# A seam of two matmul schedules reordered, kept sums weighed in pieces, and the last group's W2 sums moved from GpSimd to VectorE

## The chip, the core and the metric

The kernel runs on one core of a Trainium2 chip. Its engines work side by side, each on its own stream of instructions: TensorE (PE, the matmuls, with the loading of weights shown apart as PEld), VectorE (DVE), ScalarE (ACT), GpSimd (POOL) and SyncE (SP), which here only starts transfers (DMAs). GpSimd starts DMAs too, among them those that add what they carry to their target. The metric is the device time in microseconds (us) of one execution, as a median of several runs.

## The reference

Two layers follow each other, all in fp32. The first is attention with a polynomial sketch in place of the softmax; B, H, S, D are 4, 4, 1088, 32 and r is 8:

```python
def phi(x):                      # 64 features of a row
    a = np.einsum('rd,bhsd->bhsr', S1, x)
    b = np.einsum('rd,bhsd->bhsr', S2, x)
    return np.einsum('bhsi,bhsj->bhsij', a, b).reshape(*x.shape[:-1], r * r)
kv = np.einsum('bhsf,bhsd->bhfd', phi(k), v);  z = phi(k).sum(2)
x = (phi(q) @ kv) / (phi(q) @ z + 1e-6)        # as 4352 rows of 128
```

The second is a mixture of E = 8 experts without dropping: every row of x goes through every expert, and a matrix P (4352 x 8) weighs the results. P is the exponential of the gate's logits, normalized 8 times over experts and over rows (Sinkhorn):

```python
for e in range(E):               # w1[e]: 128 x 1024, w2[e]: 1024 x 128
    out += P[:, e:e+1] * (np.maximum(x @ w1[e], 0) @ w2[e])
```

P is never negative, so a row may be weighed before the relu (x times P) as well as after W2. The kernel uses both.

## The kernel before, in words

**Groups, items, blocks.** x lies transposed in SBUF (xT, 128 x 4352). Its columns are cut into groups (line 711), and a group with an expert is an *item*; an item is worked in *blocks*, each a share of the 1024 hidden features. The first eight groups run on experts 0 and 1 alone, unweighed, while attention and the routing are still being worked; their results are *kept* (kept0, kept1), to be weighed once P is there. Then come five groups of three tiles of 256 columns, with 7 experts each (6 for one of them), of two blocks an item, and a last group of two tiles of 256 columns, columns 0 to 511, with experts 2 to 7 and four blocks an item.

**Fewer multiplications.** Each block has two layers of matmuls, the *first products* (W1 times x, then a relu into hidden tiles hb or hx) and the *second products* (W2 times hidden, added up in four PSUM banks s). Both replace full products by fewer products of sums of their operands, and the sums are made by the other engines:
- Plain blocks (functions two, four; first products line 1058, relu on ScalarE line 1062; second products seven or twenty through into, matmul line 1434). Their sums of hidden tiles are VectorE's: lines 1077 (two tiles) and 1144 (three). In groups of two tiles, W2's sums ws (sums_of_two, lines 202 to 205) are four subtractions or additions of GpSimd per expert. In groups of three tiles W2's 20 forms are made once per expert, stored to HBM and loaded back (ws<-ws, 1280 KB).
- *New blocks* (function middle): all groups of three tiles but the first. Here the first products too work on sums: of W1 (forms wl and wf, made once per expert in forms_of_first, lines 271 to 325, and stored) and of x. A new x has two tiles, xe and de: VectorE weighs xT by a row of P spread over all partitions (px; line 806), ScalarE copies (line 815), and four adding DMAs of GpSimd join the halves (line 822; of these de<-xe and de<-de come first). A product is a *half product*: 64 rows of the array, 64 columns at a time, so that two different ones, one in the lower and one in the upper rows, run at once when they meet; a *whole* product fills all 128 rows. In a new block ScalarE copies a seed (line 1268), makes m5 (1270) and relus (1274); VectorE adds (1279).

**Order.** TensorE and VectorE, and ScalarE where the three-tile groups begin, run in the order in which the program is written (manual_schedule), up to the end of the new blocks; SyncE's transfers and GpSimd's instructions keep that order where keep_in_program_order says so, and are placed by the scheduler otherwise. Outside the new blocks the order comes from a generator (steps) that goes step by step: one step is one first product and the second products that are due, some 1.1 us in the three-tile group; beside (line 1454) hangs further work on steps c of an item, and prepare_new (line 1478) prepares the first two new items, with c counted from the first new item's start (negative is before). In the new blocks it comes from a list of jobs with planned times: block n begins at n x 8.83 (PERIOD, line 1222), and every job stands at its own time after it (FIRST, SCALAR, VECTOR, SECOND); jobs are sorted by time and written in that order. A block's second products stand some 13 to 25 us after its beginning. So at the *first seam*, in front of the new blocks, the second products of the last two plain blocks stand among the first products of the first new ones; at the *second seam*, behind them, the first products of the last group's first three blocks (EARLY) stand among the last second products. From there on the generator goes on with the last group.

**Kept outputs.** weigh_kept (line 827) is called at the beginning of an item, one part each: GpSimd weighs kept0 in pieces of 256 columns by a row of P (pb; line 771 in weigh), then kept1 if that group has it, then adds the second to the first (line 839), and for the last group subtracts one half from the other (line 842). Only the group at column 512 and the last group have a kept1. The last group's are done during the last new group.

**Forms of the next expert.** During the first three-tile group forms_of_first of the next expert is spread over the steps of an item: ScalarE copies and turns signs (line 279: turn), GpSimd adds by DMA (line 282: plus, wa<-wa and others), SyncE stores (line 285: keep_to, wf<-wa). ScalarE's turn_across at step 6 reads what the adding DMA wa<-wa brings; last_sum, the last addition, is at step 9.

## Time and profile before

Three runs took 902.21, 905.29 and 906.96 us; the median is 905.29. One more execution was profiled: it took 905.74 us, with a span of 904.0 us from first to last instruction. All times of the trace are of that one.

| | whole span | 110 to 310 us (plain blocks) | 310 to 335 (first seam) | 335 to 800 (new blocks) | 800 to 826 (second seam) | 826 to 904 (last group) |
|---|---|---|---|---|---|---|
| TensorE busy, us | 887.58 | 199.78 | 21.40 of 25 | 463.51 of 465 | 23.12 of 26 | 72.84 of 78 |
| VectorE busy | 776.84 | 167.56 | 11.06 | 440.28 | 21.86 | 52.19 |
| ScalarE busy | 551.58 | 126.69 | 11.17 | 316.70 | 11.71 | 36.41 |
| GpSimd busy | 192.50 | 23.42 | 6.88 | 108.03 | 13.20 | 17.77 |

How to read the rows of the profile: a window's row gives its length, then for PE, PEld, DVE, ACT and POOL the busy time with the count of instructions, then TensorE's granted clock (1.00 is full speed), the share of time in which the DMA engines were busy, and GB/s. A row of the timeline gives the time in the span, the duration, engine, line of the program, operation, what is written and from what, shapes, the number of instructions put together (x), and in brackets the idle time of the engine just before and what ended it. A row of the list of waits gives engine, target, line, what was waited for, and total, count and longest. SPq and POOLq rows are issues of DMAs; q1 is the queue of DMAs that SyncE starts, q0 that of GpSimd's. TensorE's busy time counts a lone half product, or two of them side by side, as busy alike.

### The profile page before, as it was taken

To read this page: it belongs to the slowest core of one execution; us is meant where nothing else is said; L and a number is where in the kernel's file an instruction comes from. 1 tells how busy PE (TensorE), PEld (TensorE's weight loads), DVE (VectorE), ACT (ScalarE), POOL (GpSimd) and SP (SyncE) were. 2 spreads that over 40 slices of the span, in tenths; PEclk is the share of its full clock that TensorE was granted. 3 is DMA by queue.
4 is the path that set the end of the run, shared out by engine and by line. 5 is a ranking of instruction groups with operands and counts; after the bars stand their busy time and mean duration, and the time that the engine had idled before them with its cause. 6 is when DMAs were issued, how large, how long until landed. Compare 5 with 4: busy or idle time off the path is not lost.

```text
span 904.0 us, 26768 instructions
## 1 busy us (share of the span) xinstructions
PE 887.6 (98%) x10934; PEld 608.3 (67%) x10934; DVE 776.8 (86%) x1525; ACT 551.6 (61%) x1251; POOL 192.5 (21%) x255
## 2 busy tenths in 40 slices
PE   8999999999999999999999999999999999999997
PEld 6777544456555447767777777777777777755775
DVE  7678689889878749999999998999989999989755
ACT  3355465576666646666767666767667676655443
POOL 3121100022111222411221221222122213132430
PEclk9999999999999999999999999999999999999999
DMA  9998200348877776865777678667776775641430
GB/s 253 304 281 291 60 1 1 88 106 235 270 206 219 204 192 183 242 189 170 189 227 214 160 178 242 203 164 205 212 187 180 228 205 154 177 149 39 124 93 13
DMA packets 84522, 159.13 MB, mean 176 GB/s; under 512 B 27936, under 2 KB 56688, under 8 KB 79552
## 3 DMA queue, kind: packets, MB, share of 16 engines
q1 hardware_dynamic: 68624, 131.39, 46.2%
q0 software_dynamic: 14544, 25.88, 15.7%
q8 instruction: 86, 1.41, 0.6%
q10 hardware_dynamic: 1232, 0.16, 0.1%
q14 instruction: 36, 0.29, 0.1%
HBM read 114.56 MB, written 25.08 MB: 154 GB/s over the span
## 4 chain that ended last, share of the span: by engine, by line
PE 55%; DVE 2%; DMA 0%; issue 0%; ACT 0%; DVEq 0%
PE a L1242 26%; PE s L1434 25%; PE a L1058 4%; DVE hb L1144 1%; DVE hx L1077 1%; DMA de<-xe 0%; DVE hx L1144 0%; DVE r L966 0%; DVE a L1279 0%; DVE m L927 0%; ACT hx L1274 0%; DVE yt L851 0%; DVE xe L806 0%; DVE x L927 0%; ACT hb L1274 0%
## 5 line engine op out<-in xcount | busy, mean ns | idle before, releaser
L1434 PE MATMUL s<-hb,ws 64*64 64x256 f32 (+4 forms) x2704 | 361.1, 385 | 2.4 <-DVE hb L1144 2.2
L1434 PE MATMUL s<-hx,ws 64*64 64x256 f32 (+1 forms) x2632 | 335.6, 378 | 0.7 <-DVE hx L1144 0.7
L1242 PE MATMUL a<-xe,w 64*64 64x384 f32 x1732 | 336.1, 484 | 0.0
L1242 PE MATMUL a<-de,w 64*64 64x384 f32 x1296 | 252.7, 483 | 3.6 <-DMA de<-de 2.1
L1434 PEld LDWEIGHTS s<-hb,ws 64*64 64x64 f32 (+1 forms) x2704 | 188.1, 134 | 85.1 <-issue 37.5
L1434 PEld LDWEIGHTS s<-hx,ws 64*64 64x64 f32 (+1 forms) x2632 | 181.7, 134 | 68.7 <-issue 20.4
L1144 DVE TENSOR_TENSOR hb<-hb 128x512 f32<-128x512 f32 (+1 forms) x340 | 190.7, 585 | 6.5 <-ACT hb L1274 2.7
L1058 PE MATMUL a<-px,w 128*64 128x256 f32 (+1 forms) x832 | 164.8, 438 | 1.5 <-ACT hx L1062 1.3
L1144 DVE TENSOR_TENSOR hx<-hx 128x512 f32<-128x512 f32 (+1 forms) x204 | 127.0, 635 | 19.4 <-ACT hx L1062 18.6
L1062 ACT ACTIVATE hb<-a 128x512 f32<-128x512 f32 (+4 forms) x192 | 88.6, 469 | 88.8 <-PE a L1058 75.8
L1242 PEld LDWEIGHTS a<-xe,w 64*64 64x64 f32 x1732 | 118.0, 133 | 24.1 <-issue 1.3
L1058 PE MATMUL a<-xT,w 128*64 128x416 f32 (+3 forms) x512 | 119.9, 463 | 0.0
L1274 ACT ACTIVATE hx<-a 128x384 f32<-128x384 f32 x162 | 76.8, 492 | 57.4 <-PE a L1242 55.3
L1274 ACT ACTIVATE hb<-a 128x384 f32<-128x384 f32 x162 | 77.1, 491 | 52.3 <-PE a L1242 48.2
L1242 PEld LDWEIGHTS a<-de,w 64*64 64x64 f32 x1296 | 89.9, 133 | 21.2 <-issue 3.1
L1058 PEld LDWEIGHTS a<-px,w 128*64 128x64 f32 x832 | 75.6, 137 | 32.1 <-issue 4.8
L1062 ACT ACTIVATE hx<-a 128x256 f32<-128x256 f32 (+1 forms) x144 | 60.9, 425 | 47.2 <-PE a L1058 43.0
L822 POOL DMA_DIRECT2D de<-xe x54 | 46.1, 1017 | 204.0 <-PE a L1242 114.1
L1077 DVE TENSOR_TENSOR hb<-hb 128x416 f32<-128x416 f32 (+7 forms) x84 | 58.7, 699 | 19.8 <-ACT hb L1062 15.7
L1279 DVE TENSOR_TENSOR a<-a,hb 128x384 f32<-128x384 f32 x108 | 60.7, 562 | 12.8 <-PE a L1242 7.6
L1270 ACT ACTIVATE hb<-a 128x384 f32<-128x384 f32 x108 | 52.9, 490 | 27.3 <-PE a L1242 27.0
L1058 PEld LDWEIGHTS a<-xT,w 128*64 128x64 f32 x512 | 49.5, 137 | 25.2 <-issue 15.5
(210 smaller groups left out, 1028.2 us busy)
## 6 DMA issues: line engine op xcount, KB each, us to landing
ws<-ws SPq DMA_DIRECT2D x34, 1280.0 KB, 6.5
w<-in_moe_w_dram SPq DMA_DIRECT2D x28, 512.0 KB, 4.7
w<-wl SPq DMA_DIRECT2D x27, 512.0 KB, 7.5
w<-wf SPq DMA_DIRECT2D x27, 512.0 KB, 9.0
px<-pT SPq DMA_DIRECT2D x34, 384.0 KB, 8.8
de<-xe POOLq DMA_DIRECT2D x27, 192.0 KB, 3.1
de<-de POOLq DMA_DIRECT2D x27, 192.0 KB, 8.4
ph<-qa SPq DMA_DIRECT2D x12, 288.0 KB, 4.7
```

Source lines behind the costliest of these rows:

```text
L822: tc.keep_in_program_order(nc.gpsimd.dma_start(out=out, in_=x, accum_op=Alu.add))
L1058: nc.tensor.matmul(ph[sl], loaded_w[j][0][:, P * f + H2 * s:P * f + H2 * (s + 1)], sources[j][:, lo:hi], start=True, stop=True, tile_posit ...
L1062: last_relu[:] = [nc.scalar.activation(out=out, in_=ph, func=Act.Relu).ins.name]
L1077: nc.vector.tensor_tensor(out, a, b, op=Alu.subtract)
L1144: nc.vector.tensor_tensor(places(out), places(a), places(b), op=Alu.subtract if off else Alu.add)
L1242: nc.tensor.matmul(out[sl], w[r, c0 + H2 * s:c0 + H2 * (s + 1)], x[r], start=start, stop=stop, tile_position=(H2 * row, H2 * s), skip_grou ...
L1270: witness(k, p, 5, nc.scalar.activation(out=m5s[p], in_=b, func=Act.Copy, scale=1.0 if p else -1.0))
L1274: ins = nc.scalar.activation(out=out, in_=x, func=Act.Relu)
L1279: ins = nc.vector.tensor_tensor(by if what == 1 else raw(k, p, 1, 1), bb[p], m5s[p], op=Alu.add)
L1434: mm = nc.tensor.matmul(sums[g][i][H2 * s:H2 * (s + 1), n * place:n * (place + 1)], w, x, start=c == (2 if t == 3 and row is None else 1) ...
```

## The change

Six things are changed.
- **First new x.** In prepare_new the first new item's row of P is fetched at step -14 in place of -10, negate stands at -13 in place of -8, and weighing, copies and joining each come four steps sooner.
- **Forms of the next expert.** turn_across moves from step 6 to 8, last_sum from 9 to 11, and the two stores from 11 and 14 to 13 and 15.
- **Second products at the first seam.** The last but one plain block had ten pairs of whole products at 0.2, 1.0, ... 7.4 us of the plan. Pairs 2, 3 and 4 become half products: the upper rows at the plan's begin, the lower ones at 6.9 to 7.3. The other seven stay whole, at times of their own.
- **Kept outputs.** weigh_kept returns a list of pieces in place of doing them all; in the new blocks they are put 3.7 us apart, in the first three-tile group at every fifth step. The addition of kept1 to kept0 is one adding DMA of GpSimd's queue over all columns. The last group's parts come one expert sooner.
- **W2's sums of the last group.** VectorE makes the four sums of each expert and weighs the first 512 columns of its x (which is all of it in the last group), in that order: weighing, then ws 0 to 3 (sums_ahead). GpSimd did both. During the last new item they stand at planned times, later at steps 8 and on of the item before. px is fetched ahead of w1 and w2. For experts 0 and 1 GpSimd keeps the sums.
- **Order.** The rest of the program, the last group with it, runs under one fixed order of TensorE, VectorE and ScalarE; before, the scheduler placed them between the new blocks and the last two blocks.

```diff
--- before.py
+++ after.py
@@ -198,11 +198,13 @@
         a12, a22 = w2[:, 1::2, 0:H2], w2[:, 1::2, H2:DM]
-        keep_ = tc.keep_in_program_order if e < 2 else lambda x: x
-        keep_(nc.gpsimd.tensor_tensor(ws[:, 0], a21, a22, op=Alu.add))
-        keep_(nc.gpsimd.tensor_tensor(ws[:, 1], ws[:, 0], a11, op=Alu.subtract))
-        keep_(nc.gpsimd.tensor_tensor(ws[:, 2], a11, a21, op=Alu.subtract))
-        keep_(nc.gpsimd.tensor_tensor(ws[:, 3], a12, ws[:, 1], op=Alu.subtract))
+        sums_ = ((0, a21, a22, Alu.add), (1, ws[:, 0], a11, Alu.subtract), (2, a11, a21, Alu.subtract),
+                 (3, a12, ws[:, 1], Alu.subtract))
+        if e > 1:
+            return ws, [lambda i=i, a=a, b=b, op=op: nc.vector.tensor_tensor(ws[:, i], a, b, op=op)
+                        for i, a, b, op in sums_]
+        for i, a, b, op in sums_:
+            tc.keep_in_program_order(nc.gpsimd.tensor_tensor(ws[:, i], a, b, op=op))
         return ws
...
@@ -321,8 +323,8 @@
-        return {-2: first_part, 2: second_part, 3: third_part, 4: fourth_part, 6: turn_across, 9: last_sum,
-                11: keep_t3, 14: keep_rest}
+        return {-2: first_part, 2: second_part, 3: third_part, 4: fourth_part, 8: turn_across, 11: last_sum,
+                13: keep_t3, 15: keep_rest}
...
@@ -745,8 +747,18 @@
             loaded_w[j] = load_w(e, not three)
+            if not three:
+                ws, own = loaded_w[j][2]
+                loaded_w[j] = *loaded_w[j][0:2], ws
+                sums_ahead[j] = [lambda: weigh_by_vector(j, slice(0, 512)), *own]
         if three:
             loaded_w[j] = *loaded_w[j][0:2], sums_of_four(e)
+
+    sums_ahead = {}
+
+    def weigh_by_vector(j, sl):
+        lo, x = groups[items[j][0]][0], sources[j]
+        nc.vector.tensor_tensor(x[:, sl], xT[:, lo:][:, sl], x[:, sl], op=Alu.mult)
...
@@ -778,7 +790,7 @@
             xe = weights_of(e, lo, t * n, "px")
-            for sl in (slice(0, 512), slice(512, 768)) if j == first_weighted else (slice(0, t * n),) if t == 2 else ():
+            for sl in (slice(0, 512), slice(512, 768)) if j == first_weighted else ():
                 weigh(xe[:, sl], x[:, sl], xe[:, sl])
...
@@ -828,18 +840,25 @@
         ys = [kept[e][:, lo:lo + n * t] for e in range(es[0])]
-        pieces = [slice(c, c + NT3) for c in range(0, n * t, NT3)]
         if i < len(ys):
-            pb = weights_of(i, lo, n * t, "pb")
-            for sl in pieces:
-                weigh(ys[i][:, sl], ys[i][:, sl], pb[:, sl])
-            return
-        for y in ys[1:]:
-            for sl in pieces:
-                tc.keep_in_program_order(nc.gpsimd.tensor_tensor(ys[0][:, sl], ys[0][:, sl], y[:, sl], op=Alu.add))
-        if t == 2:
+            pb = []
+
+            def piece(c):
+                if not c:
+                    pb.append(weights_of(i, lo, n * t, "pb"))
+                sl = slice(c, c + NT3)
+                weigh(ys[i][:, sl], ys[i][:, sl], pb[0][:, sl])
+
+            return [lambda c=c: piece(c) for c in range(0, n * t, NT3)]
+
+        def plus(y):
+            tc.keep_in_program_order(nc.gpsimd.dma_start(out=ys[0], in_=y, accum_op=Alu.add))
+
+        def less():
             k1, k2 = ys[0][upper, 0:n], ys[0][upper, n:2 * n]
             tc.keep_in_program_order(nc.gpsimd.tensor_tensor(k1, k1, k2, op=Alu.subtract))
+
+        return [lambda y=y: plus(y) for y in ys[1:]] + [less] * (t == 2)
...
@@ -1350,12 +1369,17 @@
                     for i in (j + 1, j + 2):
-                        add(t + 3.9 + 2 * PERIOD * (i - j - 1), prepare_w, i)
-                        add(t + 4 + 2 * PERIOD * (i - j - 1), prepare_x, i)
+                        at_ = t + 3.9 + 2 * PERIOD * (i - j - 1)
+                        add(at_, prepare_x, i)
+                        add(at_ + 0.1, prepare_w, i)
+                    for i, at_ in enumerate((10, WEIGH, WEIGH + 0.3, PERIOD + 10, PERIOD + WEIGH)):
+                        add(t + at_, lambda: sums_ahead[j + 1].pop(0)())
                 if 1 <= es.index(e) <= es[0] + 1:
-                    add(t + 5, weigh_kept, g, es.index(e) - 1)
-                if g == len(groups) - 2 and 4 <= es.index(e) <= 6:
-                    add(t + 5, weigh_kept, len(groups) - 1, es.index(e) - 4)
+                    for i, do in enumerate(weigh_kept(g, es.index(e) - 1)):
+                        add(t + 5 + 3.7 * i, do)
+                if g == len(groups) - 2 and 3 <= es.index(e) <= 5:
+                    for i, do in enumerate(weigh_kept(len(groups) - 1, es.index(e) - 3)):
+                        add(t + 5 + 3.7 * i, do)
             ahead = j + 2 + q
...
@@ -1380,8 +1404,11 @@
                 add(t + at_ + PERIOD, at_ease)
-        for n, i in enumerate((0, 1, 2, 5, 3, 4, 6, 7, 8, 9)):
-            add(0.2 + 0.8 * n, whole_product, ks[0] - 2, i)
+        for i in (2, 3, 4):
+            add(0.01 * i, second_product, ks[0] - 2, i, 1)
+            add(6.5 + 0.2 * i, second_product, ks[0] - 2, i, 0)
+        for i, at_ in ((0, 1.5), (1, 1.6), (5, 3), (6, 4.5), (7, 5.5), (8, 7.3), (9, 7.6)):
+            add(at_, whole_product, ks[0] - 2, i)
         for row in range(2):
...
@@ -1455,6 +1482,8 @@
         forms_at(j, c)
+        if pieces_kept and c % 5 == 1:
+            pieces_kept.pop(0)()
         if j == first_weighted and c < 6 or 9 <= c < 15 and not new_of(j + 1):
...
@@ -1466,27 +1495,24 @@
         if c in (5, 6) and not new_of(j + 1):
-            e, g = items[j + 1][1], items[j + 1][0]
-            sl = slice(0, 512) if c == 5 else slice(512, 3 * NT3)
-            x = sources[j + 1]
-            nc.vector.tensor_tensor(x[:, sl], xT[:, groups[g][0]:][:, sl], x[:, sl], op=Alu.mult)
+            weigh_by_vector(j + 1, slice(0, 512) if c == 5 else slice(512, 3 * NT3))
         if new_of(j + 1) or new_of(j + 2):
...
-    pieces = []
+    pieces, pieces_kept = [], []
...
-        if c == -8:
+        if c == -13:
             negate(items[j][0])
-        elif c == -10:
+        elif c == -14:
             fetch_weights(j)
...
             second_weights(j)
-        i, c = (j, c + 9) if c < 0 else (j + 1, c)
+        i, c = (j, c + 13) if c < 0 else (j + 1, c)
         if c in (4, 5):
...
@@ -1519,12 +1545,9 @@
                     yield 0
-                    with tc.manual_schedule(engines={engines.DVE, engines.PE, engines.Activation}):
-                        middle()
+                    middle()
                     yield 0
                 continue
-            if k == len(blocks) - 2:
-                ctx.enter_context(tc.manual_schedule(engines={engines.DVE, engines.PE, engines.Activation}))
             if k == len(blocks):
...
@@ -1541,8 +1564,8 @@
                                 prepare_w(i)
-                    if weighted and 1 <= es.index(e) <= es[0] + 1 and g < len(groups) - 1:
-                        weigh_kept(g, es.index(e) - 1)
+                    if tiles == 3 and 1 <= es.index(e) <= es[0] + 1:
+                        pieces_kept[:] = weigh_kept(g, es.index(e) - 1)
                 if j == 0 and q == 2:
...
@@ -1557,6 +1580,8 @@
                     beside(j, c + 8 * q)
+                elif k < len(blocks) and 4 * q + c > 7 and sums_ahead.get(j + 1):
+                    sums_ahead[j + 1].pop(0)()
                 if k < len(blocks) and c == 0:
...
@@ -1652,8 +1677,8 @@
                 break
-    for _ in work:
-        pass
+        for _ in work:
+            pass
...

```

## The prediction, before the changed kernel was run

> **What bounds the kernel now.** I read the page first, then busy time by windows, TensorE's waits, and the order in time on each engine at the two places where the windows show a hole.
>
> ```profile
> PE 887.6 (98%) x10934; PEld 608.3 (67%) x10934; DVE 776.8 (86%) x1525; ACT 551.6 (61%) x1251; POOL 192.5 (21%) x255
> ...
> 320.00:340.00 20.00, 17.91 (x206) 9.91 (x206) 7.76 (x16) 9.31 (x21) 4.30 (x5) 1.00 0.74 165
> ...
> 400.00:420.00 20.00, 20.00 (x312) 14.31 (x308) 19.62 (x43) 13.70 (x31) 3.39 (x4) 1.00 0.69 196
> ...
> 840.00:860.00 20.00, 20.00 (x188) 15.12 (x186) 13.10 (x19) 9.31 (x25) 9.49 (x10) 1.00 0.55 152
> ...
> PE s L1434 <- DVE hb L1144: 2.2, 2, 1.6
> PE a L1242 <- DMA de<-de: 2.1, 1, 2.1
> PE a L1058 <- ACT hx L1062: 1.3, 1, 1.3
> ```
>
> TensorE is the bound: in a whole window of the new blocks it is never idle, at the full clock (1.00). So only the holes can be won. The whole list of its waits is short, and three places hold it: the seam into the new blocks (310 to 333 us: 1.3 and 2.1), a dent near 382 (shown below), and the seam out of them (802 to 826: 2.2 and 0.7). The idle time understates the loss: 320 to 340 has 206 matmuls against 312 in a full window, because half-height products run alone there. What isn't a hole, the change can't shorten: no matmul is removed, and after the first seam TensorE's order is unchanged to the end.
>
> **First seam.** Rows of ScalarE, GpSimd, SyncE, VectorE and TensorE in order of time, and two views of the DMA queues (312 to 318 us, 286 to 335 us):
>
> ```profile
> 292.20 0.60 ACT L1062 ACTIVATE hb<-a 128x512 f32<-128x512 f32 x1 [0.28 <-PE a L1058]
> 299.76 0.50 ACT L815 COPY de<-xe 128x384 f32<-128x384 f32 x1
> 310.87 0.63 ACT L279 ACTIVATE wb<-wa 64x512 f32<-64x512 f32 x1 [3.21 <-DMA wa<-wa]
> 319.41 0.46 ACT L1268 COPY a<-a 128x384 f32<-128x384 f32 x1 [1.37 <-PE a L1242]
> 334.51 0.46 ACT L1268 COPY a<-a 128x384 f32<-128x384 f32 x1
> ...
> 300.17 0.84 POOL L282 DMA_DIRECT2D wa<-wa  x1 [7.51 <-ACT wa L279]
> 300.71 2.00 POOL L822 DMA_DIRECT2D de<-xe  x2
> 312.53 0.88 POOL L822 DMA_DIRECT2D de<-de  x1 [9.81 <-DMA de<-xe]
> ...
> 311.42 0.59 SPq L767 DMA_DIRECT2D px<-pT  x1
> 333.85 0.54 SPq L285 DMA_DIRECT2D wf<-wa  x1
> ...
> 329.94 0.55 DVE L806 TENSOR_TENSOR xe<-xT,px 128x384 f32<-128x384 f32 x1
> ...
> 316.00 0.86 PE L1242 MATMUL a<-xe,w 64*64 64x384 f32 x4
> 316.69 0.81 PE L1242 MATMUL a<-de,w 64*64 64x384 f32 x4
> ...
> q1 hardware_dynamic: 379, 1.46, 97.6%
> q0 software_dynamic: 2, 0.00, 0.3%
> ...
> px<-pT SPq DMA_DIRECT2D x4, 384.0 KB, 3.7
> ```
>
> A new block is planned at 8.83 us (PERIOD, line 1222), with one seed copy L1268 at its head; the first two stand 15.10 apart, so the first block loses 6.3 us, and 1.3 went just before it. Two causes. ScalarE stood 3.2 us on "wa<-wa" while TensorE's banks filled up: that is the 1.3. And the new x came late: its first additions were issued at 300.7 right after "wa<-wa", landed only by 312.5 (9.8 us), and the last "de<-de", issued then, held TensorE until 322.8. GpSimd's DMAs (q0) get nothing while SyncE's (q1) have data: 0.3% against 97.6%.
>
> What the change does here. (a) Weighing and copies of the first new x move four steps of 1.1 us ahead; in ScalarE's new order the last copy follows the relus at 292 and 293, so ends at 294.3 instead of 300.3, and its additions stand ahead of "wa<-wa" on GpSimd. They run in the gap before SyncE's loads of 299, the second pair at the latest when those end (308): "de" is there by 310, against a need at about 315. The 2.1 goes. (b) ScalarE's turn moves two steps (2.2 us) back, behind one 512 relu of the last block: due at 310.3, when "wa<-wa" lands. The 1.3 goes; if the landing slips to 312, some 1.0 stays. Its price elsewhere: GpSimd's last sum and the stores also move two steps; nothing waits for them before the next item. (c) The old block's products 2, 3, 4 become halves. A half product holds its half of the array 0.69 us (316.00 to 316.69). My walk through the new order leaves halves empty 0.7 (beside the first product), 0.7 and 0.7 (around product 1), 0.2, and 1.1 (three old halves in the lower rows with the upper empty): 3.4 half-us, 1.7 of the array; five changes between whole and half products at 0.15 add 0.7: 2.4 of the 6.3 stay. (d) SyncE's queue is reordered: px for the third new item, issued at 311.42 before, now stands behind the store "wf<-wa", which waits for GpSimd's last sum, itself behind the second new x's additions. These start at 309.5, are shut out while the 1280 KB of ws move (to about 316), and the sum lands some 4 us later: px leaves near 321 and lands near 325 (3.7 after issue, plus the store). VectorE wants it (the 329.94 row) 13.9 after the first new product, less 3.9 won: 314.7 + 10.0 = 324.7. Queued behind it on VectorE are the sums of the first new block, and TensorE behind those. Cost 0 to 3.5; I take 0.5, the nearest to the two times. The forms of the second new item stand behind px too: landing near 329, wanted at 333.
>
> By the Trainium skill, "DMA: Bandwidth & Descriptors", section "Queues, rings and completion order", each DMA engine takes packets in turn from the queues that have work. By that rule GpSimd's additions would get a half share, and the 0.5 would be 0. The trace disagrees (0.3% beside 97.6%), so the sum goes by the row.
>
> First seam: 1.3 + 6.3 - 2.4 - 0.5 = 4.7 us won; ends 1 and 7.
>
> **New blocks.** ScalarE's seed copies, GpSimd and VectorE:
>
> ```profile
> 378.79 0.46 ACT L1268 COPY a<-a 128x384 f32<-128x384 f32 x1 [0.21 <-PE a L1242]
> 389.68 0.46 ACT L1268 COPY a<-a 128x384 f32<-128x384 f32 x1 [0.25 <-PE a L1242]
> ...
> 354.49 3.29 POOL L771 TENSOR_TENSOR kept<-kept,hb 128x256 f32<-128x256 f32 x3 [11.04 <-DMA hb<-pT]
> 379.82 3.41 POOL L839 TENSOR_TENSOR kept<-kept,kept 128x256 f32<-128x256 f32 x3
> ...
> 377.27 0.42 DVE L966 TENSOR_TENSOR r<-z,m 64x256 f32<-64x256 f32 x1
> 379.46 2.73 DVE L966 TENSOR_TENSOR r<-r 64x256 f32<-64x256 f32 x1
> ```
>
> While GpSimd adds, a VectorE instruction of 0.42 takes 2.73, and the block 10.89 instead of 8.83. The three additions become one DMA of 384 KB on GpSimd's queue, whose next work comes 13 us later: 2.06 us won. The weighing in pieces wins nothing here: its three instructions still stand one behind the other on GpSimd with one wait ahead, and no order ties them to other engines, so they run together as at 354.49. Sum 2.1; ends 1.5 and 3.
>
> **Second seam.** VectorE, GpSimd, TensorE, and one window:
>
> ```profile
> 790.99 1.89 DVE L1144 TENSOR_TENSOR hb<-hb 128x512 f32<-128x512 f32 x3
> 799.35 0.57 DVE L1279 TENSOR_TENSOR a<-a,hb 128x384 f32<-128x384 f32 x1 [1.14 <-ACT hx L1274]
> 800.85 2.89 DVE L1144 TENSOR_TENSOR hx<-hx 128x512 f32<-128x512 f32 x2
> 816.45 3.77 DVE L1144 TENSOR_TENSOR hb<-hb 128x512 f32<-128x512 f32 x3
> 820.14 2.82 DVE L1077 TENSOR_TENSOR hx<-hx 128x512 f32<-128x512 f32 x3
> ...
> 798.27 0.73 POOL L202 TENSOR_TENSOR ws<-w 128x256 f32<-128x256 f32 x1 [15.41 <-DMA w<-in_moe_w_dram]
> 852.86 0.72 POOL L202 TENSOR_TENSOR ws<-w 128x256 f32<-128x256 f32 x1 [5.99 <-DMA w<-in_moe_w_dram]
> ...
> 823.35 2.39 PE L1434 MATMUL s<-hb,ws 64*64 64x256 f32 x24 [1.56 <-DVE hb L1144]
> 843.42 0.38 PE L1058 MATMUL a<-px,w 128*64 128x256 f32 x1
> 856.37 0.38 PE L1058 MATMUL a<-px,w 128*64 128x256 f32 x1
> ...
> 800.00:810.00 10.00, 9.32 (x117) 5.48 (x111) 8.96 (x13) 4.01 (x10) 6.45 (x6) 1.00 0.15 36
> ```
>
> Three sums take 1.89 alone, 3.77 beside GpSimd's W2 sums; two take 2.89 for 1.3; three smaller ones 2.82 for 1.4. TensorE waits for these sums, and all of GpSimd's arithmetic leaves this place. VectorE gets one 512 and four 256 pieces an item instead, 0.60 + 4 x 0.34 = 2.0 us (steps from 1.89 for three; a 256 has a bit over half of that). For the first item 1.3 of it stands ahead of the 799.35 instruction, where VectorE was idle 1.14; in the last group it is busy 13.1 of 20 and can take it. Of the first burst TensorE lost 0.7 (its wait) to 2.5: 117 matmuls in 800 to 810 where a full window has 156 in ten. 16 of the 117 fill twice the array, so 1.5 is left; I take 1.9, between 1.5 and 2.5. The later waits, 0.6 and 1.6, go; 0.4 comes back, because the sums still start behind the last relu. 1.9 + 2.2 - 0.4 = 3.7; ends 1.5 and 6. The bunched sums of the last new group are spread; TensorE was full from 826 on, so that wins nothing.
>
> The added wait: VectorE stands on each item's w2. It landed at 798.27 (the row) against a turn near 798.4: even; px now goes ahead of it, up to 3.7 later, which would hold the last block's sums. In the last group it lands 9.4 us into an item of 12.95; VectorE's turn is step 9 of 16, 7.3: 2.1 us of waiting, ahead of nothing due before step 12 (9.7) and used before step 16. Hidden; I take 0.
>
> **Sum.** 4.7 + 2.1 + 3.7 = 10.5 off 904.0: 893.5. The profiled execution took 905.74 with 1.74 outside the span, 0.45 above the median of 905.29: 895.2. A difference under 0.5% (4.5 us) is no difference here.
>
> **Rivals.** (1) SyncE's queue decides: px and the second item's forms land past 328, the first seam wins 1: 898.9. For it: px sits behind a wait for GpSimd; against: 3 us too late is needed. (2) The second seam wins little: w2 lands 3.7 later than before, in front of the last block's sums, and 3.5 come back: 898.7. For it the 15.41 wait; against, the bytes ahead of w2 are the same px that shared its transfer. (3) Slower: VectorE's wait for w2 in the last group falls on the path. Slack from 9.4 to the use is about 2.6 us; each us beyond is paid in four items. If w2 lands 6.5 later than now, 4 x 3.9 = 15.6: 911. Against: the buffer is freed by TensorE as before. (4) All holes but the run-out close: 890. (5) The pieces do come apart and spare the bursts that remain: 893.3; counted with the forecast.
>
> **How the numbers follow.** Forecast 0.56, (4) 0.06, (1) 0.16 with a third of it above 900.8, (2) 0.12 with 0.05 of it there, (3) 0.10. Faster 0.80, same 0.10, slower 0.10. The forecast's own ends are 891.5 and 898.5; the range, 890 to 900.5, leaves out (3) and the tails of (1) and (2).
>
> **What will show it.** Right: the first two L1268 about 11.5 apart; no ScalarE wait on "wa<-wa"; the block at 379 back at 8.83; bursts like 354.49 unchanged; after 798 no GpSimd arithmetic and three 512 sums in 1.9. Wrong: VectorE waiting on "px<-pT" or "w<-in_moe_w_dram", with TensorE behind it.

## The result, and the profile after

The changed kernel took 901.17 us (median; 900.1 to 903.7), the kernel before, beside it, 906.26: a ratio of 0.994, 95% interval 0.9924 to 0.9955. It is faster by some 5 us where 10.5 were forecast, and the predicted time, 895.2, is missed by 6.0. The profiled execution had a span of 898.2 us against 904.0. Among the runs with a mean granted clock of 0.999 or 1.000 the medians are 904.06 (33 of the 72 runs of the kernel before that stood beside the experiments) and 900.80 (11 of 20), 3.3 apart, so a part of the 5 lies in runs at a lower clock.

The gain is told by stages, from the two profiles. M is TensorE's first product of the three-tile groups, B the seed copy that opens the second new block, C the one that opens the last new block. The rows of M and C in the timelines of the kernel before and of the changed one (B before was the 334.51 row; new line numbers: 1058 is 1077, 1268 is 1287, 1434 is 1461; rows between those shown are left out):

```profile
184.57 0.59 PE L1058 MATMUL a<-px,w 128*64 128x512 f32 x1
...
797.44 0.46 ACT L1268 COPY a<-a 128x384 f32<-128x384 f32 x1 [0.25 <-PE a L1242]
```
```profile
184.14 0.59 PE L1077 MATMUL a<-px,w 128*64 128x512 f32 x1
...
317.27 0.46 ACT L1287 COPY a<-a 128x384 f32<-128x384 f32 x1 [0.21 <-PE a L1261]
...
333.04 0.46 ACT L1287 COPY a<-a 128x384 f32<-128x384 f32 x1
...
794.77 0.46 ACT L1287 COPY a<-a 128x384 f32<-128x384 f32 x1 [0.25 <-PE a L1261]
```

| stage, us | before | after | difference | forecast |
|---|---|---|---|---|
| start to M | 184.57 | 184.14 | -0.4 | 0 |
| M to B (first seam) | 149.94 | 148.90 | -1.0 | -4.7 |
| B to C (new blocks) | 462.93 | 461.73 | -1.2 | -2.1 |
| C to the end of the span (second seam) | 106.56 | 103.43 | -3.1 | -3.7 |

The first line is no gain: in the fourteen profiles of this document M lies between 184.1 and 186.2, and none of them touches what comes before it. What is short is the first seam. Its rows in the timeline after (ScalarE, TensorE, GpSimd, SyncE, VectorE), then TensorE's waits, then the queues and issues of 314 to 318 us (KB, us from issue to landing):

```profile
311.83 0.63 ACT L281 ACTIVATE wb<-wa 64x512 f32<-64x512 f32 x1 [2.00 <-DMA wa<-wa]
...
330.83 0.51 ACT L827 COPY de<-xe 128x384 f32<-128x384 f32 x1 [4.85 <-DVE xe L818]
331.25 0.48 ACT L1293 ACTIVATE hx<-a 128x384 f32<-128x384 f32 x1
...
313.13 1.94 PE L1077 MATMUL a<-px,w 128*64 128x512 f32 x12 [1.35 <-ACT hb L1081]
...
298.84 0.89 POOL L834 DMA_DIRECT2D de<-de  x1 [3.63 <-DMA de<-xe]
299.95 1.56 POOL L284 DMA_DIRECT2D wa<-wa  x1
309.02 1.64 POOL L834 DMA_DIRECT2D de<-xe  x2 [3.66 <-ACT de L827]
314.39 0.90 POOL L834 DMA_DIRECT2D de<-de  x1 [3.73 <-DMA de<-xe]
315.51 1.56 POOL L284 DMA_DIRECT2D wa<-wb  x1
...
324.29 0.53 SPq L287 DMA_DIRECT2D wf<-wa  x1
324.87 0.60 SPq L779 DMA_DIRECT2D px<-pT  x1
...
330.24 0.56 DVE L818 TENSOR_TENSOR xe<-xT,px 128x384 f32<-128x384 f32 x1 [5.00 <-DMA px<-pT]
```
```profile
PE a L1261 <- ACT hx L1293: 1.9, 1, 1.9
PE a L1077 <- ACT hb L1081: 1.4, 1, 1.4
```
```profile
q1 hardware_dynamic: 117, 1.10, 89.0%
...
wa<-wb POOLq DMA_DIRECT2D x1, 256.0 KB, 8.8
de<-de POOLq DMA_DIRECT2D x1, 192.0 KB, 7.9
```

The wait for "de<-de" is gone. Two others are there. ScalarE still stands 2.00 us for wa<-wa, and TensorE 1.35 behind it. And px for the third new item, on SyncE's queue behind the store wf<-wa, was issued at 324.87 and held VectorE for 5.00 us, until 330.24. ScalarE, whose fixed order has the copy of this xe next, stood 4.85 us behind VectorE, and the relu behind the copy (the 331.25 row) released TensorE after 1.9. The store had waited for GpSimd's last sum, wa<-wb, issued at 315.51 and 8.8 us on its way. From 314 to 318 GpSimd's queue moved nothing (only q1 has a row), with de<-de issued at 314.39 and wa<-wb behind it. The first two blocks stand 15.77 apart (317.27 to 333.04), no better than the 15.10 before.

In the new blocks, GpSimd's rows; at the second seam, VectorE's, and a window that before had 117 matmuls and 6.45 us of GpSimd:

```profile
352.91 3.50 POOL L783 TENSOR_TENSOR kept<-kept,hb 128x256 f32<-128x256 f32 x3 [10.82 <-DMA hb<-pT]
370.10 2.56 POOL L783 TENSOR_TENSOR kept<-kept,hb 128x256 f32<-128x256 f32 x3 [2.89 <-DMA hb<-pT]
378.74 1.55 POOL L855 DMA_DIRECT2D kept<-kept  x1
```
```profile
807.62 1.89 DVE L1163 TENSOR_TENSOR hb<-hb 128x512 f32<-128x512 f32 x3 [2.25 <-ACT hb L1293]
...
860.33 0.43 DVE L204 TENSOR_TENSOR ws<-w 128x256 f32<-128x256 f32 x1 [0.45 <-DMA w<-in_moe_w_dram]
```
```profile
800.00:810.00 10.00, 9.39 (x128) 5.79 (x122) 7.71 (x17) 4.53 (x12) 0.00 (x0) 1.00 0.43 129
```

The pieces of weighing still run three in a row; the addition is a DMA. Three sums take 1.89 in the last block too, and GpSimd does no arithmetic there. In the sequence of seed copies the block at 379 is whole again (8.84, before 10.89). Two others now lose: the one ahead of it, with a burst of weighing (9.15, before 8.84), and the one at 741, where weighing for the last group falls since its parts come one expert sooner (9.28, before 8.86).

### The profile page after: what moved, and what is told of

It reads as the page before. It is cut to its first block, busy times and chain, and to the rows that moved or that the text cites. A ratio compares the mean times of both kernels' runs of the same rounds, so it can differ in the third digit from the quotient of the medians.

```text
span 898.2 us, 26769 instructions
## 1 busy us (share of the span) xinstructions
PE 886.7 (99%) x10946; PEld 616.8 (69%) x10946; DVE 773.8 (86%) x1555; ACT 553.3 (62%) x1251; POOL 161.3 (18%) x222
## 4 chain that ended last, share of the span: by engine, by line
PE 95%; DMA 2%; DVE 2%; ACT 0%; issue 0%; POOL 0%; SPq 0%; DVEq 0%; POOLq 0%
PE s L1461 40%; PE a L1261 29%; PE a L1077 21%; PE a L427 1%; DMA wa<-wb 1%; PE a L542 1%; PE a L114 1%; DMA px<-pT 1%; DMA de<-xe 0%; PE a L394 0%; PE s L456 0%; DVE hb L1096 0%; PE a L506 0%; PE s L472 0%; PE a L576 0%
## 5 line engine op out<-in xcount | busy, mean ns | idle before, releaser
L1461 PE MATMUL s<-hb,ws 64*64 64x256 f32 (+4 forms) x2704 | 379.0, 385 | 1.5 <-ACT hx L1293 0.6
L1461 PE MATMUL s<-hx,ws 64*64 64x256 f32 (+1 forms) x2644 | 351.7, 378 | 0.0
L1461 PEld LDWEIGHTS s<-hb,ws 64*64 64x64 f32 (+1 forms) x2704 | 197.7, 134 | 77.7 <-issue 25.2
L1461 PEld LDWEIGHTS s<-hx,ws 64*64 64x64 f32 (+1 forms) x2644 | 190.8, 134 | 59.8 <-issue 6.6
L1163 DVE TENSOR_TENSOR hb<-hb 128x512 f32<-128x512 f32 (+1 forms) x340 | 188.2, 577 | 10.0 <-ACT hb L1081 6.6
L1077 PE MATMUL a<-px,w 128*64 128x256 f32 (+1 forms) x832 | 189.0, 437 | 1.4 <-ACT hb L1081 1.4
L1163 DVE TENSOR_TENSOR hx<-hx 128x512 f32<-128x512 f32 (+1 forms) x204 | 125.6, 628 | 14.2 <-ACT hx L1081 12.5
L1077 PEld LDWEIGHTS a<-px,w 128*64 128x64 f32 x832 | 94.0, 137 | 38.3 <-issue 2.7
```

The source lines that it names most:

```text
L1077: nc.tensor.matmul(ph[sl], loaded_w[j][0][:, P * f + H2 * s:P * f + H2 * (s + 1)], sources[j][:, lo:hi], start=True, stop=True, tile_posit ...
L1163: nc.vector.tensor_tensor(places(out), places(a), places(b), op=Alu.subtract if off else Alu.add)
L1461: mm = nc.tensor.matmul(sums[g][i][H2 * s:H2 * (s + 1), n * place:n * (place + 1)], w, x, start=c == (2 if t == 3 and row is None else 1) ...
```

## The experiments

Each kernel ran beside the kernel before. "M to B" and the like are stages of its profile, as above. The theory to be tried: px, pushed behind a store that waits for a slow sum, is what the first seam lost.

**px ahead.** One transfer of the changed kernel moves: from the plan of the new blocks to step 15 of the last plain item.

```diff
-        add(0.3, fetch_weights, first_new + 2)
...
+        if c == 15 and new_of(j + 1):
+            fetch_weights(first_new + 2)
         forms_at(j, c)
```


> The changed kernel with one transfer moved: px for the third new item is put on SyncE's queue ahead of the last two stores of forms (step 15 of the last plain item), where the changed kernel has it behind them. In the changed kernel px was issued at 324.87 and landed at 330.21; VectorE stood 5.00 us for it and TensorE 1.95 behind VectorE. Theory (late px): px leaves when TensorE has read its buffer for the last time, near 315, and lands by 320; VectorE's wait goes, the first two seed copies stand 12 to 12.5 apart in place of 15.78, and the time falls by 3.3 from 901.2 to 897.9. Rival (the new order of products at the seam loses this time by itself, and px was only the last to be waited for): the copies stay 14.5 or more apart, the time falls by 1 at most, 900.2. A third outcome: px takes the DMA engines from the stores and sums, and something else is late by as much: no change, 901.2.

898.38 us (897.59 to 899.39), 2.8 below the changed kernel, with no overlap of the runs. ScalarE, SyncE, VectorE, TensorE:

```profile
312.74 0.63 ACT L281 ACTIVATE wb<-wa 64x512 f32<-64x512 f32 x1 [2.46 <-DMA wa<-wa]
318.18 0.46 ACT L1287 COPY a<-a 128x384 f32<-128x384 f32 x1 [0.21 <-PE a L1261]
...
331.62 0.46 ACT L1287 COPY a<-a 128x384 f32<-128x384 f32 x1
...
314.55 0.92 SPq L779 DMA_DIRECT2D px<-pT  x1
...
326.05 0.55 DVE L818 TENSOR_TENSOR xe<-xT,px 128x384 f32<-128x384 f32 x1
...
314.04 1.94 PE L1077 MATMUL a<-px,w 128*64 128x512 f32 x12 [1.82 <-ACT hb L1081]
```

px is issued 10 us sooner, VectorE's row has no wait, the blocks stand 13.44 apart, and M to B falls from 148.90 to 147.03. The theory holds: 2.8 us by the medians where 3.3 were expected. The rest of the seam is somewhat worse than it said (13.4 where 12 to 12.5 were expected).

**The order by itself, from both sides.** First the changed kernel with its last part undone, then the kernel before with that part alone:

```diff
-                    middle()
+                    with tc.manual_schedule(engines={engines.DVE, engines.PE, engines.Activation}):
+                        middle()
...
+            if k == len(blocks) - 2:
+                ctx.enter_context(tc.manual_schedule(engines={engines.DVE, engines.PE, engines.Activation}))
...
-        for _ in work:
-            pass
+    for _ in work:
+        pass
```


> The changed kernel with the last part of the change alone undone: the new blocks stand in an ordered region of their own again, and the last group outside it. In the program that comes out, px for the third new item stands ahead of the ws load and of the stores on SyncE's queue, as in the kernel before. Theory (late px): px is issued near 312 again, VectorE does not wait for it, and the first seam wins what it wins with px moved by hand, 3.3: 897.9, give or take 1 for the last group, where the scheduler orders VectorE and ScalarE again. Rival (the seam's products lose it by themselves): 900.2 to 901.2.

912.79 us (911.74 to 913.72). SyncE, then VectorE:

```profile
313.67 0.59 SPq L779 DMA_DIRECT2D px<-pT  x1
...
795.45 1.35 DVE L761 TENSOR_TENSOR px<-xT,px 128x512 f32<-128x512 f32 x2 [6.66 <-DMA px<-pT]
...
817.52 0.42 DVE L204 TENSOR_TENSOR ws<-w 128x256 f32<-128x256 f32 x1 [4.94 <-DMA w<-in_moe_w_dram]
```

px leaves at 313.67 and M to B is 147.14, as with px moved by hand: the first seam went by the theory. The total did not, since VectorE now stands 6.66 and 4.94 us for the last group's px and w2, and TensorE 6.5 and 3.5 behind it, each time with TensorE's granted clock at 0.50 for some us behind it (*half clock* below; shown at the end of this section): B to C 470.47, C to the end 108.3.

> The kernel before with the last part of the change alone: one ordered region from the plain blocks to the end of the last group. On SyncE's queue px for the third new item then stands behind the last store of forms, which waits for wa<-wb; in the kernel before that addition landed at 333.83, and px was wanted at 329.9. Theory (the fixed order by itself puts px there): px lands near 339, the first two seed copies stand 20 or more apart in place of 15.10, and the time rises by 5 to 7, less up to 1.5 that the order may win in the last group: 908 to 911. Rival (px's place comes from another part of the change): 904 to 905.5, no change.

911.13 us (909.04 to 913.35), ratio 1.0054 (1.0025 to 1.0083). SyncE, VectorE, ScalarE:

```profile
329.18 0.53 SPq L285 DMA_DIRECT2D wf<-wa  x1
329.75 0.60 SPq L767 DMA_DIRECT2D px<-pT  x1
...
334.97 0.56 DVE L806 TENSOR_TENSOR xe<-xT,px 128x384 f32<-128x384 f32 x1 [6.56 <-DMA px<-pT]
...
319.96 0.46 ACT L1268 COPY a<-a 128x384 f32<-128x384 f32 x1 [1.37 <-PE a L1242]
...
337.78 0.46 ACT L1268 COPY a<-a 128x384 f32<-128x384 f32 x1
```

The fixed order alone puts px behind the store (311.42 before, 329.75 now) and the blocks 17.82 apart. TensorE stood 4.5 us, and half clock followed. So it is this part of the change that put px late and lost time at the first seam; undone as above, it cost more in the last group than it gave back.

**Forms' times back.**

```diff
-        return {-2: first_part, 2: second_part, 3: third_part, 4: fourth_part, 8: turn_across, 11: last_sum,
-                13: keep_t3, 15: keep_rest}
+        return {-2: first_part, 2: second_part, 3: third_part, 4: fourth_part, 6: turn_across, 9: last_sum,
+                11: keep_t3, 14: keep_rest}
```


> The changed kernel with the times of the next expert's forms as before (turn across at step 6, last sum at 9, stores at 11 and 14). Theory: ScalarE meets the landing of wa<-wa at 311.75 two steps sooner and stands 3.5 to 4 us in place of 2.0; TensorE waits about 3 in place of 1.35 in front of the seam. px is no sooner, since the last sum stands behind the second new x's additions on GpSimd in either case, and TensorE has to wait for px at 330.2 anyhow, which hides most of it: 901.2 to 902. Rival (the stores come two steps sooner, and with them px): 899 to 900. Second rival (nothing hides the longer wait): 903.

906.67 us (903.55 to 908.09): worse than every expectation. ScalarE, SyncE and VectorE:

```profile
312.10 0.63 ACT L281 ACTIVATE wb<-wa 64x512 f32<-64x512 f32 x1 [3.95 <-DMA wa<-wa]
...
329.53 0.60 SPq L779 DMA_DIRECT2D px<-pT  x1
...
335.01 0.56 DVE L818 TENSOR_TENSOR xe<-xT,px 128x384 f32<-128x384 f32 x1 [7.55 <-DMA px<-pT]
```

ScalarE stood 3.95 us for wa<-wa, its copies of the second new x and so the additions came late (issued 314.24, not 309.02), and the last sum, the store and px with them. The longer wait wasn't hidden; it went down the same chain, to a wait of TensorE of 4.5 us in place of 1.9, with half clock behind it.

**The turn two steps later,** with px ahead: in every item (first diff), and in the last plain item alone (second):

```diff
-        return {-2: first_part, 2: second_part, 3: third_part, 4: fourth_part, 8: turn_across, 11: last_sum,
-                13: keep_t3, 15: keep_rest}
+        return {-2: first_part, 2: second_part, 3: third_part, 4: fourth_part, 10: turn_across, 13: last_sum,
+                14: keep_t3, 15: keep_rest}
```
```diff
-        forms_at(j, c)
+        forms_at(j, {8: 7, 10: 8}.get(c, c) if new_of(j + 1) else c)
```


> px for the third new item ahead of the last two stores, and ScalarE's turn across moved on from step 8 to 10 (last sum to 13, first store to 14). With px moved alone ScalarE stood 2.46 us for wa<-wa, which landed at 312.66, and TensorE 1.8 behind it. Theory: two steps later the turn stands behind two more relus and is due after the landing; TensorE's 1.8 goes, and nothing takes its place: 896.6. Rival: the wait is only handed on, since TensorE reaches the first new products sooner and then stands for the new x or for the relus behind the turn: 898.0.

900.35 us (898.88 to 902.01). Moved everywhere, the wait was handed on as the rival had it: TensorE stood 2.2 us for a relu in place of 1.82. But M to B grew by 2.5, to 149.49, and the time went above the rival's 898.0. The larger part of that is not the wait: behind it TensorE's granted clock was 0.50 for 3.4 us.

> px for the third new item ahead of the last two stores, and the turn across at step 10 in the last plain item alone; the other items keep it at 8, and all other forms stay where they are. Moving the turn and the last sum in every item handed the wait on: ScalarE then stood 2.79 us for wa<-wb an item earlier step, and VectorE 4.79 for the second px. Theory: in the last plain item wa<-wa lands near 312.5, the turn is due near 312, TensorE's 1.8 in front of the seam goes: 896.8 against 898.4 with px moved alone. Rival: TensorE comes to the seam sooner, and px, the second new x or a relu is late by as much: 898.

897.12 us (896.48 to 898.3), the fastest kernel of the study, ratio 0.9887 to before (0.9847 to 0.9927). ScalarE:

```profile
313.18 0.63 ACT L281 ACTIVATE wb<-wa 64x512 f32<-64x512 f32 x1 [0.76 <-DMA wa<-wa]
...
317.45 0.46 ACT L1287 COPY a<-a 128x384 f32<-128x384 f32 x1 [0.55 <-PE a L1261]
...
330.87 0.46 ACT L1287 COPY a<-a 128x384 f32<-128x384 f32 x1
```

TensorE waits no more behind the turn. M to B is 145.33: 4.6 below the kernel before.

**The first new x at its old times,** with px ahead.

```diff
-        if c == -13:
+        if c == -8:
             negate(items[j][0])
-        elif c == -14:
+        elif c == -10:
...
-        i, c = (j, c + 13) if c < 0 else (j + 1, c)
+        i, c = (j, c + 9) if c < 0 else (j + 1, c)
```


> px for the third new item ahead of the last two stores, and the first new x at its old times, four steps later. Theory (the prediction's first step): its additions are issued behind wa<-wa at 300.7 and the second pair only when the first has landed at 312.5; TensorE stands 2.1 us for de<-de again, and the second new x's additions are late too: 900.5 to 901.5 against 898.4. Rival: with px in time the seam has no use for the sooner x: 898.4.

901.64 us (900.05 to 904.33). A line of TensorE's waits, then GpSimd and ScalarE:

```profile
PE a L1261 <- DMA de<-de: 2.1, 1, 2.1
```
```profile
301.61 0.84 POOL L284 DMA_DIRECT2D wa<-wa  x1 [6.20 <-ACT wa L281]
314.03 0.89 POOL L834 DMA_DIRECT2D de<-de  x1 [9.88 <-DMA de<-xe]
...
311.92 0.63 ACT L281 ACTIVATE wb<-wa 64x512 f32<-64x512 f32 x1
```

The 2.1 is back to the tenth. But TensorE's 1.82 behind the turn is gone, and M to B is the same (147.15, 147.03): at the seam the two waits trade places. B to C is 1.0 longer; that and M, which came 1.6 later in this profile by nothing that was edited, is all the profile shows of the 3.3 us between the medians; the rest stays open.

**Halves against whole pairs.** The ten whole pairs of the kernel before, first with px late (the diff), then with px ahead; then, on the fastest kernel, halves for pair 2 alone (second diff):

```diff
-        for i in (2, 3, 4):
-            add(0.01 * i, second_product, ks[0] - 2, i, 1)
-            add(6.5 + 0.2 * i, second_product, ks[0] - 2, i, 0)
...
+        for n, i in enumerate((0, 1, 2, 5, 3, 4, 6, 7, 8, 9)):
+            add(0.2 + 0.8 * n, whole_product, ks[0] - 2, i)
```
```diff
+        add(0.02, second_product, ks[0] - 2, 2, 1)
+        add(6.9, second_product, ks[0] - 2, 2, 0)
+        for i, at_ in ((0, 1.0), (1, 1.8), (5, 2.6), (3, 3.4), (4, 4.2), (6, 5.0), (7, 5.8), (8, 6.6), (9, 7.4)):
             add(at_, whole_product, ks[0] - 2, i)
```


> The changed kernel with the second products at the first seam as in the kernel before: ten whole pairs, none as halves. Theory (late px): TensorE stands behind VectorE until px has landed at 330.2 whatever it has done until then, so the halves are worth little as long as px is late: 901.2 to 901.9. Rival (the halves win what the prediction gave them, 2 to 3 us, and the px wait stands beside that): 903 to 904. Third: the halves cost time in themselves, 900 or less.

901.4 us (898.6 to 904.64), M to B 149.07 against 148.90: worth nothing measurable with px late.

> px for the third new item ahead of the last two stores, and the second products at the first seam as ten whole pairs again. With px early and halves the time was 898.38, with px late and whole pairs 901.4, with both as changed 901.17. Theory: px late hid what the order of the products is worth; with px in time the halves win against whole pairs what the prediction gave them, some 2 us: the first two seed copies about 15 apart in place of 13.45, 900.5. Rival: the halves never win anything here, since each leaves the other half of the array empty as long as a whole product would take: 13.5 apart, 898.4 as with halves.

899.21 us (898.83 to 900.74), M to B 147.97 against 147.03: with px in time the halves win 0.8 to 0.9, between theory and rival; the runs of the two overlap (898.38, 897.59 to 899.39, with halves).

> As the kernel with the turn across at step 10 in the last plain item, and of the ten pairs of second products only pair 2 as halves; the rest are whole, 0.8 us apart. In the profile with px moved alone the lower halves of three pairs stood without partners near 326 to 328 and cost 1.0 us there; whole pairs alone cost time at the seam's begin. Theory: one pair of halves keeps the gain at the begin without the lone halves: 0.5 to 1 faster than the kernel with three pairs of halves. Rival: the places where TensorE waits move along, and the sum stays within 0.5.

898.18 us (897.43 to 900.47), M to B 146.6 against 145.33: 1.1 slower, so the theory falls. That the lone halves cost less than what three pairs of halves win is an inference; the profile shows 0.5 of the 1.3 ahead of the first seed copy and 0.8 behind it.

**W2's sums on GpSimd again,** at the same places of the program.

```diff
-            return ws, [lambda i=i, a=a, b=b, op=op: nc.vector.tensor_tensor(ws[:, i], a, b, op=op)
+            return ws, [lambda i=i, a=a, b=b, op=op: nc.gpsimd.tensor_tensor(ws[:, i], a, b, op=op)
...
-                sums_ahead[j] = [lambda: weigh_by_vector(j, slice(0, 512)), *own]
+                sums_ahead[j] = [lambda: weigh(sources[j], xT[:, groups[g][0]:][:, 0:512], sources[j]), *own]
```


> The changed kernel with the W2 sums and the weighing of the last group given back to GpSimd, at the places where VectorE has them. Theory: GpSimd's arithmetic doubles VectorE's sums at the second seam again and TensorE loses there what it lost before, 7.9 against 4.7 us: 3.2 slower, 904.4. Rival: the second seam was won by the fixed order alone, and GpSimd's arithmetic costs nothing there: 901.2 to 902.

903.15 us (901.45 to 906.38). GpSimd and VectorE:

```profile
814.69 0.91 POOL L204 TENSOR_TENSOR ws<-ws,w 128x256 f32<-128x256 f32 x1
...
814.94 3.77 DVE L1163 TENSOR_TENSOR hb<-hb 128x512 f32<-128x512 f32 x3
```

The 3.77 is back, and 2.0 us (1.6 in the stage: C to the end 105.0 against 103.4), where 3.2 were expected. Where the other 1.5 of the second seam's 3.1 comes from stays open. The fixed order alone hardly brings it: C to the end is 109.5 in the kernel before with that part, and still some 106.1 without what half clock cost there (3.4, estimated below), against 106.56. The 108.3 of VectorE's sums without that order is no test of it, since 3.5 of it is the wait behind w2 and some 1.7 half clock.

**The kept sums added by GpSimd again.**

```diff
-            tc.keep_in_program_order(nc.gpsimd.dma_start(out=ys[0], in_=y, accum_op=Alu.add))
+            for c in range(0, n * t, NT3):
+                sl = slice(c, c + NT3)
+                tc.keep_in_program_order(nc.gpsimd.tensor_tensor(ys[0][:, sl], ys[0][:, sl], y[:, sl], op=Alu.add))
```


> The changed kernel with the addition of kept1 to kept0 as three GpSimd additions of 256 columns again (two for the last group), at the place of the adding DMA. Theory: the block during them lasts 10.9 in place of 8.83 us, and the last group's additions cost some 0.3: 2.1 to 2.4 slower, 903.4. Rival: the block in which they fall now has slack, and they cost no more than the bursts of weighing, 0.5: 901.7.

904.35 us (902.71 to 906.05), 3.2 slower. Their block took 9.89 (378.89 to 388.78) where before it had taken 10.89, and B to C grew by 1.5; the rest lies at the first seam (0.6) and ahead of M (0.8), where the edit does nothing. At the first seam TensorE stood 2.3 us behind the turn, with half clock after it, which has nothing to do with the additions. So the DMA wins some 1.5, not 2.06.

**What the stages also hold: the granted clock.** In five of these profiles TensorE's granted clock falls to 0.50 for a few microseconds, from the end of an idle stretch or shortly before or behind it. The same 16 products in front of the first seam, in the kernel before and with the turn two steps later everywhere:

```profile
313.27 2.80 PE L1058 MATMUL a<-px,w 128*64 128x512 f32 x16 [0.24 <-ACT hb L1062]
```
```profile
312.87 0.65 PE L1077 MATMUL a<-px,w 128*64 128x256 f32 x4 [2.23 <-ACT hx L1081]
313.76 4.38 PE L1077 MATMUL a<-px,w 128*64 128x512 f32 x16 [0.24 <-ACT hb L1081]
```

They take 4.38 us in place of 2.80. The table has all such places from M to the last 3 us of a span; the loss is an estimate, half of TensorE's busy time at that clock.

| kernel | TensorE idle, us (until) | clock 0.50 from, to | loss, us |
|---|---|---|---|
| px ahead, turn at 10 everywhere | 2.23 (312.87) | 313.6, 317.0 | 1.6 |
| kept sums by GpSimd | 2.29 (314.88) | 314.6, 318.0 | 1.6 |
| forms' times back | 4.50 (336.56) | 336.0, 339.4 | 1.4 |
| kernel before, one region | 4.50 (336.52) | 337.2, 340.6 | 1.7 |
| the same, last group | 1.55 (827.42) | 828.7, 835.6 | 3.4 |
| changed kernel, two regions | 6.48 (797.32) | 794.2, 801.0 | 1.8 |
| the same, last group | 3.47 (819.90) | 821.5, 824.9 | 1.7 |

The profiles of the kernel before, of the changed one and of the fastest have no such place, though idle stretches there reach 2.09. So for these five kernels a stage, and probably the median, holds not only what the edit cost but also what the clock took behind it; stages without such a place can be compared as they are.

## Why the prediction was wrong, step by step

- **TensorE bounds, only holes can be won: right.** Every difference was found at the two seams and in single blocks.
- **(a), the first new x sooner: the wait as said, the gain not.** The 2.1 for de<-de went, and came back to the tenth when undone. But its additions now stand ahead of wa<-wa on GpSimd's queue and (b) pays for it: with px in time M to B was the same with and without (a).
- **(b), the 1.3 goes: wrong.** The prediction named the condition ("if the landing slips to 312, some 1.0 stays"). It happened: ScalarE's row at 311.83 is where wa<-wa landed, and 1.35 stayed. Already before the change the landing was at 310.9 and not at 310.3. (a) and (b) had been summed as if apart, though they draw on one queue. Two steps more in the last plain item gave 1.3 (medians) to 1.7 (stage).
- **(c), the walk: right in sum, by luck, and not in its parts.** In the fastest kernel the first block keeps 4.6 of lost time (13.42 less 8.83) and not 2.4, but it opens 2.9 us sooner after M than before (131.9 against 134.8), and not 1.3. There M to B won 4.6 against a forecast of 4.7. Of the forecast's terms, halves against whole pairs were measured alone: 0.8 to 0.9 with px in time.
- **(d), the order of SyncE's queue: the step that failed.** The place was right, and so were the chain that delays px and the time at which it is needed: with px ahead, VectorE took it 10.1 after the first new product (forecast 10.0). Behind VectorE the way was another: TensorE waited for ScalarE's copy and the relu behind it, and not for VectorE's sums. And the size was wrong: px left at 324.87, not 321, and landed 5.3 later, not 3.7. The sum before it is a chain of two rounds: the first additions landed before 314.39, but the second round and the last sum, issued then, moved nothing until 318 while ws and the stores behind it did, and needed 7.9 and 8.8 us. Of the ends 0 to 3.5 the prediction took 0.5; 1.9 (stage) to 2.8 (medians) were lost. This is rival (1), px past 328 and a seam that wins 1, which was given 0.16. The rule of the Trainium skill weighed there ("DMA: Bandwidth & Descriptors", "Queues, rings and completion order") would have had q0 take turns. The changed kernel's trace shows both: no packet of q0 in 314 to 318 beside 89% of q1, which speaks against it again, but 197 packets of q0 beside 208 of q1 in 304 to 309 (31.4% and 74.9% of the engines), which is what turns by the packet would give. The row on which the sum relied, 0.3% beside 97.6%, holds for its own window and not as a rule.
- **New blocks: 2.1 was too much.** The block at 379 won its 2.05, but the block ahead of it lost 0.31 and the one at 741 lost 0.42, for which the forecast had no term: B to C won 1.2, below the ends of 1.5 to 3. Alone, the additions by DMA are worth 1.5.
- **Second seam: the size right, the cause in part.** 3.1 of 3.7, the sums at 1.89, VectorE's wait for w2 in the last group hidden, as forecast (0.45 in the row above; 2.1 had been expected). But GpSimd's arithmetic was half of it and not all. One reading was off: the window's 117 matmuls hold 11 whole products and not 16, which makes its lower end 1.8 and not 1.5.
- **The range** (890 to 900.5) ended just below the result because it was made up of cases that miss one term; here three terms fell short together, the first by 3.7. Of these 3.7, (d) has 1.9 and (b) 1.7 by the stages of the experiments.

## What to carry to other kernels

When two ordered regions become one, read the order of the transfer queues as well as that of the engines: a load that used to slip ahead can come to stand behind a store that waits for a slow sum. Two waits that end with transfers of the same queue are one term, not two: what is put ahead of the one delays the other. Compare stages between fixed marks, since a stretch that no edit touches moved by 2 us from profile to profile, as much as most edits here are worth. And look at the granted clock behind every hole: a longer wait can cost its own length and some 1.5 us more.

## What the hardware showed unexpectedly

Additions on GpSimd's DMA queue that were issued at 314.39 and 315.51, while SyncE's queue had data, had moved nothing by 318 and took 7.9 and 8.8 us to land; those issued at 309.02 were done by 314.39. Some of the delay is there without any rival: additions issued at 356.35, with idle DMA engines, moved their first packet 1.4 us later. The two queues don't always exclude each other, as 304 to 309 shows; what decides it was not tried.

And px, 384 KB spread over all partitions, needed 5.3 us from issue to landing where the median before the change had been 3.7 in this stretch.

From M on, TensorE's granted clock was 0.50 at the end of, or soon behind, every idle stretch of 2.2 us and more in the fourteen profiles (2.23 to 6.48), for 3.4 or 6.8 us, and stayed at 1.00 behind those of 2.0 to 2.1 us. Length alone doesn't decide it: in one profile it also fell behind 1.55 us, for 6.8.
